# Attention plus mixture of experts on one core: the last unconditional slot computes its fourth feature block in two token parts

## The chip, the cores and the metric

The kernel runs on one core of one Trainium2 chip. The metric is the device time of one launch in microseconds (us), the median of the runs of the kernel. The engines are PE (TensorE, matmuls; PEld is its weight loading), ACT (ScalarE), DVE (VectorE), POOL (GpSimd, which here issues the indirect DMAs) and SP (which issues the plain DMAs). Each engine works through its own instructions in the order in which they were written; engines wait for each other through semaphores.

## The reference

```
scores = q @ k.T / sqrt(64) + bias(position)        # 4 batches, 8 heads, 576 tokens
x = softmax(scores) @ v  ->  (2304 tokens, 512 features)
e_idx = argmax(x @ w_gate)                          # one of 8 experts for each token
h  = relu(x[mask] @ w1[e])                          # 512 -> 1024
ye = h @ w2[e]                                      # 1024 -> 512
out[mask] = gate_w * sigmoid(x @ w_output_gate)[e] * ye
```

## The kernel before

The first 345 us or so are the attention. The rest, which the change touches, is the mixture of experts. Tokens of one expert are put into slots of CH = 288 tokens, in three groups of G = 96. SURE = 8 slots (0 to 7) are run unconditionally, by `body(s)`; further ones stand behind conditions and do not run with this input. FIRST_FEW is a small rest of 32 tokens that is computed beside slot 7.

`body(s)` has two phases. In the first, f runs over 8 blocks of 128 hidden features: 12 matmuls each (L1104), over c = 0 to 3 the pairs (w1h[c], xh), (w1h[c], xl), (w1l[c], xh). A weight is split into a rounded part and a remainder in the fp32r format: `split` lets ACT cast (L484) and then DVE subtract (L485). So the first f block reads w1h[3] in its 10th matmul and w1l[3] in its 12th. In the second phase d runs over 4 blocks of 128 output features, 24 matmuls of 288 columns each (L1125); ACT copies the block from PSUM to yt (L1131). During block d of slot s also the weight tile d of the next slot is split, and in d = 1 and 2 the next slot's tokens are transposed on PE (L513), cast on ACT (L514) and subtracted on DVE (L515).

After the four blocks the slot's answer is turned to token rows: 12 transposes (L1144) into three PSUM tiles pt, one for each group, the blocks d = 0 to 2 first, then d = 3. The tiles are copied to y by DVE, ACT, DVE (L1147) and scattered to `out` by POOL (`put`, L1069). Slot 7 writes its rows into xg[1], and its three scatters are issued at the very end of the program, groups in the order 1, 0, 2, behind the scatter of the few. PSUM tiles of the tag t (`psum_t`) rotate through three buffers; so a transpose waits until the third tile before it was read.

`slot_work` runs leftover work of the attention inside the first slots. In slot 0 this is at d = 2 and d = 3 one step each of `emit_x`: four transposes (L655) into one psum_t tile and one DVE multiplication (L664) that empties it. The third pt tile of slot 0's answer takes the buffer of the second of these.

Of the kernel before, what the change touches and what calls it, by code (L numbers as in the profile page):

```python
# [9 lines left out]
F32 = mybir.dt.float32  # L10
# [17 lines left out]
CH = 288  # L28
G = 96
# [4 lines left out]
SURE_A, SURE = 6, 8  # L34
# [98 lines left out]
def attention_moe_kernel(  # L133
# [15 lines left out]
    nc = tc.nc  # L149
    V = nc.vector  # L150
# [19 lines left out]
    def cn(name):  # L170
        o, n = _WHERE[name]
        return kept[:, o:o + n]

    ident = cn("ident")
# [8 lines left out]
    def psum_t():  # L183
        return ps_t[-1].tile([128, 512], F32, name="pt", tag="t")
# [288 lines left out]
    def load_w1(s):  # L473
        src = mw1[bass.ds(expert(s), 1)].rearrange("o (c p) f -> p (o c) f", p=128)
        for i in range(4):
            nc.sync.dma_start(out=w1r[i], in_=src[:, i, :])

    def load_w2(s):
        src = mw2[bass.ds(expert(s), 1)].rearrange("o (c p) f -> p (o c) f", p=128)
        for i in range(4):  # L480
            nc.sync.dma_start(out=w2r[i], in_=src[:, 2 * i:2 * i + 2, :])

    def split(hi, lo, src):
        nc.scalar.copy(out=hi, in_=src)  # L484
        V.tensor_tensor(out=lo, in0=src, in1=hi.bitcast(F32), op=ALU.subtract)  # L485

    def side(s):

        return s % 2 if s < SURE else 0

    def gather(s):
        part = int(s >= SURE_A)
        for j in range(1 if s == FIRST_FEW else 3):
            g = 3 * s + j
            nc.gpsimd.indirect_dma_start(
                out=xg[side(s)][j], out_offset=None, in_=x_dram[:, :] if part else x_dram[0:(B - 1) * S, :],
                in_offset=bass.IndirectOffsetOnAxis(ap=gidx[part][:, g:g + 1], axis=0),
            )

    def transpose_few():  # L500
        pt = psum_t()
        for c in range(4):
            nc.tensor.transpose(
                pt[:, c * G:c * G + G], xg[0][0][:, c * 128:c * 128 + 128], ident[0:G, 0:G]
            )
        V.tensor_copy(out=few[0], in_=pt[:, 0:4 * G].rearrange("p (c g) -> p c g", g=G)[:, :, 0:FEW])

    def transpose_x(s, c):
        xh, xl = xs[side(s)]
        xg_s = xg[side(s)]  # L510
        pt = psum_t()
        for j in range(3):
            nc.tensor.transpose(pt[:, j * G:j * G + G], xg_s[j][:, c * 128:c * 128 + 128], ident[0:G, 0:G])  # L513
        nc.scalar.copy(out=xh[:, c, :], in_=pt[:, 0:CH])  # L514
        V.tensor_tensor(out=xl[:, c, :], in0=pt[:, 0:CH], in1=xh[:, c, :].bitcast(F32), op=ALU.subtract)  # L515
        if s >= SURE:
            V.tensor_copy(out=few[0][:, c, :], in_=pt[:, 0:FEW])
# [154 lines left out]
    with ExitStack() as actx:  # L672
# [12 lines left out]
        o, n = _WHERE["psi"]  # L685
        early = hb.tile([128, 144 + 36], F32, name="early", bufs=1)
        bc, cinv = early[:, 0:144], early[:, 144:180]
        ot, n = _WHERE["tab"]
# [277 lines left out]
        for hl in range(2):  # L966
            for i, w in enumerate((wg, wog)):
                nc.sync.dma_start(
                    out=wgb[hl * 64:hl * 64 + 64, :, hl * 16 + i * 8:hl * 16 + i * 8 + 8],
                    in_=w.rearrange("(a t d) e -> t d a e", t=2, d=64)[hl],  # L970
# [24 lines left out]
        for n in range(len(pairs) + 1):  # L995
            for op in orders.get(n, ORDER).split():
                name = op.rstrip("+-")
# [54 lines left out]
    with ExitStack() as ctx:  # L1052
# [3 lines left out]
        ps2 = ctx.enter_context(tc.tile_pool(name="ps2", bufs=2, space=PSUM))  # L1056

        w2h = [wr.tile([128, 2, DM], F32R, name=f"w2h{i}") for i in range(4)]
        w2l = [wr.tile([128, 2, DM], F32R, name=f"w2l{i}") for i in range(4)]
        hh_all, hl_all = (hp.tile([128, 8, CH], F32R, name=t) for t in ("hh", "hl"))  # L1060
        hh, hl = ([t[:, i, :] for i in range(8)] for t in (hh_all, hl_all))
# [5 lines left out]
        def put(s, j, y, n=G):  # L1067
            idx = sidx[int(s >= SURE_A)][0:n, 3 * s + j:3 * s + j + 1]
            p = nc.gpsimd.indirect_dma_start(  # L1069
                out=out, out_offset=bass.IndirectOffsetOnAxis(ap=idx, axis=0),  # L1070
                in_=y[0:n], in_offset=None, bounds_check=NTOK - 1, oob_is_err=False,
            )
            for other in puts:
                tc.declare_no_dep(p.ins, other.ins, reason="no row of the answer is written twice")
            puts.append(p)
# [4 lines left out]
        def new_y(s, j):  # L1080

            if s == SURE - 1:
                return xg[1][j]
            return y2 if j == 2 else x_p.tile([128, DM], F32, name="y", tag="x")[0:G]

        def slot_work(s, at):
            for w in SLOT_WORK[s].split() if s < len(SLOT_WORK) else ():
                if w == at:
                    do_work()

        def after(s, n):

            return None if s >= SURE else s + n if s + n < SURE else FIRST_FEW if s + n == SURE else None

        def body(s):
            assert s < 5 or not (work or rows)
            xh, xl = xs[side(s)]
            for f in range(8):
                fs = slice(f * 128, f * 128 + 128)
                p1 = ps1.tile([128, 512], F32, name="p1", tag="p1")  # L1100
                n = 0
                for c in range(4):
                    for w, x in ((w1h[c], xh), (w1h[c], xl), (w1l[c], xh)):
                        nc.tensor.matmul(p1[:, 0:CH], lhsT=w[:, fs], rhs=x[:, c, :], start=n == 0, stop=n == 11)  # L1104
                        n += 1
                nc.scalar.activation(out=hh[f], in_=p1[:, 0:CH], func=ACTF.Relu)  # L1106
                V.scalar_tensor_tensor(  # L1107
                    out=hl[f], in0=p1[:, 0:CH], scalar=0.0, in1=hh[f].bitcast(F32), op0=ALU.max, op1=ALU.subtract
                )
                if f % 2 == 0:  # L1110
                    i = f // 2
                    split(w2h[i], w2l[i], w2r[i])
                slot_work(s, "f%d" % f)
            if after(s, 1):
                load_w2(after(s, 1))
            yt = yts[s % 2]
            if after(s, 1) == FIRST_FEW:
                transpose_few()
            for d in range(4):
                ds = slice(d * 128, d * 128 + 128)  # L1120
                p2 = ps2.tile([128, 512], F32, name="p2", tag="p2")
                n = 0
                for f in range(8):
                    for w, x in ((w2h, hh), (w2h, hl), (w2l, hh)):
                        nc.tensor.matmul(  # L1125
                            p2[:, 0:CH], lhsT=w[f // 2][:, f % 2, ds], rhs=x[f], start=n == 0, stop=n == 23
                        )
                        n += 1
                if after(s, 1) == s + 1:
                    split(w1h[d], w1l[d], w1r[d])  # L1130
                nc.scalar.copy(out=yt[:, d, :], in_=p2[:, 0:CH])  # L1131
                if after(s, 1) == s + 1 and d in (1, 2):
                    for c in (2 * d - 2, 2 * d - 1):
                        transpose_x(s + 1, c)
                if after(s, 1) == FIRST_FEW and d < 3:
                    (few_hidden, few_turn, few_last)[d]()
                slot_work(s, "d%d" % d)
            if after(s, 2):
                load_w1(after(s, 2))
            pts = [psum_t() for j in range(3)]  # L1140
            for d0, d1 in ((0, 3), (3, 4)):
                for j, pt in enumerate(pts):
                    for d in range(d0, d1):
                        nc.tensor.transpose(pt[0:G, d * 128:d * 128 + 128], yt[:, d, j * G:j * G + G], ident)  # L1144
            for j, pt in enumerate(pts):
                y = new_y(s, j)
                (V.tensor_copy, nc.scalar.copy, V.tensor_copy)[j](out=y, in_=pt[0:G, :])  # L1147
                if s != SURE - 1:
                    put(s, j, y)
            if after(s, 2):  # L1150
                gather(after(s, 2))

        few_h, few_ht = (yts[0].rearrange("p a b -> p (a b)")[:, 256 * i:256 * i + 256] for i in range(2))

# [43 lines left out]
        def either(s):  # L1198
            flag = ns + 1 + s
            is_small = nc.values_load(seq[int(s >= SURE_A)][0:1, flag:flag + 1], min_val=0, max_val=1)  # L1200
            with tc.If(is_small > 0) as cmp:
                small(s)
            with cmp.Else():
                body(s)

        for s in range(SURE):
            body(s)
# [44 lines left out]
```

## Time and profile before

| what | value |
|---|---|
| median of 3 runs | 593.14 us (593.07 to 593.64) |
| profiled execution, its own time | 593.73 us |
| its span in the trace | 591.9 us |
| mean granted TensorE clock (share of full speed) | 0.996 |

The span is the time between the first and the last instruction that the profiler saw; 1.8 us of the execution lie around it. Times in rows are microseconds from the start of the span.

### The profile page before, as it was taken

The page shows a single profiled execution, that of the slowest core. Times are in us where ns is not written, and L with a number is a line of the kernel's source. Part 1 is how long each engine was busy: PE and PEld are TensorE (multiplying, and loading weights), DVE is VectorE, ACT ScalarE, POOL GpSimd, SP SyncE. Part 2 cuts the span into 40 slices and gives each one's busy share as a digit, 9 for nine tenths or more (in the row PEclk, how much of TensorE's full clock was granted, in tenths as well). Part 3 has the DMA queues.
Part 4 walks back from the last instruction along what each step waited for, and adds up shares of the span by engine and source line. Part 5 has one row for each costly group of instructions (what it writes and reads, how often), then busy time and mean ns, then how long its engine had stood idle before and what let it go on. Part 6 is the DMA issues. An engine that isn't in the chain of part 4 may idle for free.

```text
span 591.9 us, 13980 instructions
## 1 busy us (share of the span) xinstructions
PE 567.2 (96%) x5294; PEld 473.7 (80%) x5294; DVE 395.7 (67%) x935; ACT 374.2 (63%) x813; POOL 106.1 (18%) x220
## 2 busy tenths in 40 slices
PE   4999899999999999999999999999999999999993
PEld 2454577777787777787787779999999999999993
DVE  5999655666866667765889846767877765565511
ACT  5998767877777777677767845444555454555411
POOL 1000111110011111011214570221222314040302
PEclk9999999999999999999999999999999999999998
DMA  6979633333224333322333765684748485766521
GB/s 136 216 205 214 164 79 71 72 72 71 49 61 114 72 72 71 112 63 48 72 102 71 264 194 172 191 263 160 232 137 245 138 246 159 208 186 211 168 69 48
DMA packets 94998, 81.41 MB, mean 138 GB/s; under 512 B 71319, under 2 KB 71575, under 8 KB 94920
## 3 DMA queue, kind: packets, MB, share of 16 engines
q1 hardware_dynamic: 88932, 66.05, 41.9%
q0 software_dynamic: 3232, 9.64, 5.2%
q10 hardware_dynamic: 2756, 4.72, 2.2%
q8 instruction: 44, 0.72, 0.5%
q14 instruction: 34, 0.28, 0.1%
HBM read 60.34 MB, written 9.50 MB: 118 GB/s over the span
## 4 chain that ended last, share of the span: by engine, by line
PE 87%; ACT 3%; DMA 3%; DVE 2%; issue 2%; SPq 1%; POOL 0%; POOLq 0%; ACTq 0%; DVEq 0%
PE p L1104 17%; PE p L1125 16%; PE pa L917 14%; PE ps L832 12%; PE pt L885 11%; PE pb L736 4%; PE pt L809 3%; PE pt L897 2%; PE pt L655 2%; DMA bias<-evh 2%; PE pt L1144 1%; PE pt L513 1%; PE pt L586 1%; ACT evh L740 1%; ACT hid L723 1%
## 5 line engine op out<-in xcount | busy, mean ns | idle before, releaser
L844 DVE CUSTOM_DVE_ANT_0 e<-ps,bias 128x576 f32<-128x576 f32 x144 | 103.9, 753 | 55.2 <-PE ps L832 51.3
L849 ACT ACTIVATE e<-e,nm 128x576 f32<-128x576 f32 x144 | 111.1, 775 | 13.6 <-DVE nm L844 13.5
L1104 PE MATMUL p<-x,w 128*128 128x288 f32 x768 | 105.8, 297 | 0.0
L1104 PEld LDWEIGHTS p<-x,w 128*128 128x128 f32 x768 | 102.8, 188 | 0.5 <-issue 0.4
L885 PE MATMUL pt<-kept,e 128*128 128x128 f32 x576 | 79.1, 278 | 0.8 <-ACT et L889 0.4
L1125 PE MATMUL p<-hh,w2h 128*128 128x288 f32 x256 | 77.3, 302 | 0.0
L889 ACT COPY et<-pt 128x512 f32<-128x512 f32 (+1 forms) x110 | 57.1, 554 | 31.8 <-PE pt L885 31.6
L1125 PE MATMUL p<-hl,w2h 128*128 128x288 f32 x256 | 75.6, 295 | 0.1
L1125 PE MATMUL p<-hh,w2l 128*128 128x288 f32 x256 | 75.3, 294 | 0.0
L917 PE MATMUL pa<-et,vt 128*64 128x256 f32 (+1 forms) x640 | 73.3, 354 | 0.2 <-DVE xt L918 0.2
L885 PEld LDWEIGHTS pt<-kept,e 128*128 128x128 f32 x576 | 63.1, 141 | 10.3 <-issue 4.4
L917 PEld LDWEIGHTS pa<-et,vt 128*64 128x64 f32 x640 | 42.9, 137 | 21.7 <-issue 7.3
L736 PE MATMUL pb<-hid,w2blk 128*32 128x288 f32 x576 | 49.5, 430 | 9.0 <-DVE hid L725 7.7
L1069 POOL DMA_INDIRECT out_dram<-y,sidx x22 | 26.3, 1198 | 173.5 <-DVE y L1147 147.2
L1106 ACT ACTIVATE hh<-p 128x288 fp32r<-128x288 f32 x64 | 26.3, 412 | 45.4 <-PE p L1104 29.5
L725 DVE TENSOR_SCALAR hid<-e,early 128x576 f32<-128x576 f32 x108 | 47.3, 514 | 4.1 <-ACT early L705 2.3
L736 PEld LDWEIGHTS pb<-hid,w2blk 128*32 128x32 f32 x576 | 22.8, 113 | 32.9 <-DVE hid L725 10.8
L485 DVE TENSOR_TENSOR w2l<-w2r,w2h 128x1024 fp32r<-128x1024 f32 x32 | 39.2, 1226 | 14.2 <-ACT w2h L484 12.7
L1125 PEld LDWEIGHTS p<-hh,w2h 128*128 128x128 f32 x256 | 48.0, 188 | 0.6 <-issue 0.6
L1125 PEld LDWEIGHTS p<-hl,w2h 128*128 128x128 f32 x256 | 48.1, 188 | 0.3 <-DVE hl L1107 0.3
L1125 PEld LDWEIGHTS p<-hh,w2l 128*128 128x128 f32 x256 | 48.2, 188 | 0.0
L832 PE MATMUL ps<-qt 64*128 64x288 f32 x256 | 46.4, 344 | 1.5 <-DVE qs L814 1.2
(222 smaller groups left out, 956.7 us busy)
## 6 DMA issues: line engine op xcount, KB each, us to landing
w1r<-in_moe_w_dram SPq DMA_DIRECT2D x36, 512.0 KB, 5.1
w2r<-in_moe_w_dram SPq DMA_DIRECT2D x36, 512.0 KB, 4.9
bias<-evh SPq DMA_DIRECT2D x16, 288.0 KB, 4.6
bias<-evl SPq DMA_DIRECT2D x16, 288.0 KB, 4.0
vt<-in_v_dram SPq DMA_DIRECT2D x16, 288.0 KB, 3.5
nat<-in_k_dram SPq DMA_DIRECT2D x32, 128.0 KB, 3.6
nat<-in_q_dram SPq DMA_DIRECT2D x32, 128.0 KB, 3.2
x_dram<-x ACTq DMA_DIRECT2D x12, 256.0 KB, 2.1
```

Source lines behind the costliest of these rows:

```text
L485: V.tensor_tensor(out=lo, in0=src, in1=hi.bitcast(F32), op=ALU.subtract)
L725: V.tensor_scalar(out=to, in0=src, scalar1=bc[:, r:r + 1], scalar2=0.0, op0=ALU.add, op1=ALU.max,)
L736: nc.tensor.matmul(pb[32 * t:32 * t + 32, c, 0:288], lhsT=w2f, rhs=hids[t][:, c * 288:c * 288 + 288], start=True, stop=True,)
L832: nc.tensor.matmul(outs[hl][:, c, 0:288], lhsT=qs[p, S + 64 + qb * 128:S + 192 + qb * 128] if qb < 4 else q4[:, t, :], rhs=keys[p, c * 288 ...
L844: V.tensor_tensor_reduce(out=e.rearrange("p (a j) -> p a j", a=2), in0=ps[:, :, 0:n], in1=bias_ap.rearrange("p (a j) -> p a j", a=2), scal ...
L849: nc.scalar.activation(out=e, in_=e, func=ACTF.Exp, scale=-1.0, bias=nm, accum_out=sum_ap)
L885: nc.tensor.transpose(pt[:, n * 256 + j * 128:n * 256 + j * 128 + 128], es[j][:, (n0 + n) * 128:(n0 + n) * 128 + 128], ident,)
L889: copy(out=et[:, n0:n0 + nn, :].rearrange("p n s -> p (n s)"), in_=pt[:, 0:nn * 256])
L917: nc.tensor.matmul(pa[p:p + 64, 0:n], lhsT=values, rhs=weights, start=i == 0, stop=i == 4)
L1069: p = nc.gpsimd.indirect_dma_start(out=out, out_offset=bass.IndirectOffsetOnAxis(ap=idx, axis=0), in_=y[0:n], in_offset=None, bounds_check ...
L1104: nc.tensor.matmul(p1[:, 0:CH], lhsT=w[:, fs], rhs=x[:, c, :], start=n == 0, stop=n == 11)
L1125: nc.tensor.matmul(p2[:, 0:CH], lhsT=w[f // 2][:, f % 2, ds], rhs=x[f], start=n == 0, stop=n == 23)
```

## The change

In slot 7 (SURE - 1) the block d = 3 is computed in two parts, first the tokens 0 to 191 (groups 0 and 1), then the tokens 192 to 287 (group 2). Between the parts the rows of groups 0 and 1 are transposed, and copied by ACT and DVE. The third group follows the second part, its copy moves from DVE to ACT. Transposing and copying are now the functions `turn` and `keep`.

A second thing changes in every slot: the copy of p2 to yt moved into the loop over the parts, which stands ahead of `split(w1h[d], ...)`; before, it stood behind it.

```
             for d in range(4):
                 ds = slice(d * 128, d * 128 + 128)
-                p2 = ps2.tile([128, 512], F32, name="p2", tag="p2")
-                n = 0
-                for f in range(8):
-                    for w, x in ((w2h, hh), (w2h, hl), (w2l, hh)):
-                        nc.tensor.matmul(
-                            p2[:, 0:CH], lhsT=w[f // 2][:, f % 2, ds], rhs=x[f], start=n == 0, stop=n == 23
-                        )
-                        n += 1
+                parts = (slice(0, 2 * G), slice(2 * G, CH)) if s == SURE - 1 and d == 3 else (slice(0, CH),)
+                for cols in parts:
+                    p2 = ps2.tile([128, 512], F32, name="p2", tag="p2")
+                    width = cols.stop - cols.start
+                    n = 0
+                    for f in range(8):
+                        for w, x in ((w2h, hh), (w2h, hl), (w2l, hh)):
+                            nc.tensor.matmul(
+                                p2[:, 0:width], lhsT=w[f // 2][:, f % 2, ds], rhs=x[f][:, cols],
+                                start=n == 0, stop=n == 23,
+                            )
+                            n += 1
+                    nc.scalar.copy(out=yt[:, d, cols], in_=p2[:, 0:width])
+                    if cols.stop == 2 * G:
+                        turn(yt, 0, 3)
+                        turn(yt, 3, 4, (0, 1))
+                        keep(s, (1, 0))
                 if after(s, 1) == s + 1:
                     split(w1h[d], w1l[d], w1r[d])
-                nc.scalar.copy(out=yt[:, d, :], in_=p2[:, 0:CH])
...
+            if s == SURE - 1:
+                turn(yt, 3, 4, (2,))
+                keep(s, (2,))
+            else:
+                turn(yt, 0, 3)
+                turn(yt, 3, 4)
+                keep(s, (0, 1, 2))
...
+        def turn(yt, d0, d1, groups=(0, 1, 2)):
+            if d0 == 0:
+                pts[:] = [psum_t() for j in range(3)]
+            for j in groups:
+                for d in range(d0, d1):
+                    nc.tensor.transpose(pts[j][0:G, d * 128:d * 128 + 128], yt[:, d, j * G:j * G + G], ident)
+
+        def keep(s, groups):
+            for j in groups:
                 y = new_y(s, j)
+                copy = V.tensor_copy if j == 0 or j == 2 and s != SURE - 1 else nc.scalar.copy
+                copy(out=y, in_=pts[j][0:G, :])
                 if s != SURE - 1:
                     put(s, j, y)
```

This is ACT's order in the second phase of slot 0, both kernels in one piece (w_0 is w1h, w1r the loaded weight, ytqt the tile yt, p the PSUM tile of a block).

```order
-L484 CAST w_0_4772<-w1r_4632 128x1024
-L1131 COPY ytqt_5119<-p_5387 128x288
-L514 CAST x<-pt 128x288 x2
-L484 CAST w_0_4772<-w1r_4633 128x1024
-L1131 COPY ytqt_5119<-p_5433 128x288
+L1133 COPY ytqt_5119<-p_5387 128x288
+L484 CAST w_0_4772<-w1r_4632 128x1024
+L514 CAST x<-pt 128x288 x2
+L1133 COPY ytqt_5119<-p_5433 128x288
+L484 CAST w_0_4772<-w1r_4633 128x1024
```

Each copy of a block moved ahead of the cast of the weight tile with the same d; the last cast now stands behind the last block's copy. The slots 1 to 6 have the same difference.

This is DVE's order at the end of slot 0 in the changed kernel (w_1 is w1l, ytqs<-pt the two steps of `emit_x`, y the rows of slot 0); apart from line numbers it is the same as before.

```order
L485 TENSOR_TENSOR w_1_4773<-w1r_4632,w_0_4772 128x1024
L515 TENSOR_TENSOR x<-pt,x 128x288 x2
L664 TENSOR_TENSOR ytqs_5120<-pt,rec 128x512
L485 TENSOR_TENSOR w_1_4773<-w1r_4633,w_0_4772 128x1024
L664 TENSOR_TENSOR ytqs_5120<-pt,rec 128x512
L1171 COPY y<-pt 96x512
L1171 COPY y_5122<-pt 96x512
L1107 SCALAR_TENSOR_TENSOR hl<-p_5514,hh 128x288
```

Nothing moved here: the subtraction that follows the last cast still stands ahead of the second L664.

This is PE's order in the changed kernel around the second part of block 3 of slot 7 (p_7878 and p_7920 are the PSUM tiles of the two parts, ytqs the tile yt).

```order
L1128 MATMUL p_7878<-hl,w2h_5112 128x192
L1128 MATMUL p_7878<-hh,w2l_5116 128x192
L1165 MATMUL pt<-kept,ytqs_5120 96x128 x11
L1128 MATMUL p_7920<-hh,w2h_5109 128x96
L1128 MATMUL p_7920<-hl,w2h_5109 128x96
...
L1128 MATMUL p_7920<-hl,w2h_5112 128x96
L1128 MATMUL p_7920<-hh,w2l_5116 128x96
L1165 MATMUL pt<-kept,ytqs_5120 96x128
```

Where 24 matmuls of 288 columns stood ahead of 12 transposes, there are 24 of 192, 11 transposes, 24 of 96 and one transpose.

## Rows read from the trace of the kernel before

**Rows 1.** Page, part 1: busy time and share of each engine.

```profile
PE 567.2 (96%) x5294; PEld 473.7 (80%) x5294; DVE 395.7 (67%) x935; ACT 374.2 (63%) x813; POOL 106.1 (18%) x220
```

**Rows 2.** Page, part 4: chain that ended last, share of the span.

```profile
PE 87%; ACT 3%; DMA 3%; DVE 2%; issue 2%; SPq 1%; POOL 0%; POOLq 0%; ACTq 0%; DVEq 0%
```

**Rows 3.** Windows: one middle slot (stretch, its length, busy time and count).

```profile
410.15:438.07 27.92, 27.92 (x218) 27.91 (x218) 20.85 (x53) 14.18 (x26) 7.21 (x6) 1.00 0.63 198
```

**Rows 4.** Timeline, end of slot 6: start, length, engine, line, operation.

```profile
538.36 0.40 ACT L1131 COPY ytqt<-p 128x288 f32<-128x288 f32 x1 [1.85 <-PE p L1125]
538.66 1.05 ACT L484 CAST w<-w1r 128x1024 fp32r<-128x1024 f32 x1
539.74 1.23 DVE L485 TENSOR_TENSOR w<-w1r,w 128x1024 fp32r<-128x1024 f32 x1 [1.97 <-ACT w L484]
...
546.14 1.07 ACT L484 CAST w<-w1r 128x1024 fp32r<-128x1024 f32 x1
...
548.99 0.40 ACT L1131 COPY ytqt<-p 128x288 f32<-128x288 f32 x1 [1.77 <-PE p L1125]
...
550.02 13.04 PE L1104 MATMUL p<-x,w 128*128 128x288 f32 x96
550.08 1.28 DVE L1147 COPY y<-pt 96x512 f32<-96x512 f32 x2 [1.61 <-PE pt L1144]
```

**Rows 5.** Timeline in slot 0: a matmul that waits for DVE.

```profile
366.10 0.45 DVE L1107 SCALAR_TENSOR_TENSOR hl<-p,hh 128x288 fp32r<-128x288 f32 x1
...
366.60 0.19 PEld L1125 LDWEIGHTS p<-hl,w2h 128*128 128x128 f32 x1 [0.32 <-DVE hl L1107]
...
366.84 0.29 PE L1125 MATMUL p<-hh,w2l 128*128 128x288 f32 x1
```

**Rows 6.** Timeline, end of slot 0 (from the answers for PE, ACT and DVE).

```profile
378.01 0.60 PE L655 MATMUL pt<-kept,xt 128*128 128x128 f32 x4
378.45 1.81 PE L1144 MATMUL pt<-kept,ytqt 128*96 128x128 f32 x12
380.01 0.77 PE L1104 MATMUL p<-x,w 128*128 128x288 f32 x4
...
378.21 0.40 ACT L1131 COPY ytqt<-p 128x288 f32<-128x288 f32 x1 [2.19 <-PE p L1125]
...
378.65 0.69 DVE L664 TENSOR_TENSOR ytqs<-pt,rec 128x512 f32<-128x512 f32 x1 [1.28 <-PE pt L655]
```

**Rows 7.** Timeline, block 3 of slot 7 and the end.

```profile
577.10 0.19 PEld L1125 LDWEIGHTS p<-hh,w2h 128*128 128x128 f32 x1 [0.20 <-issue]
...
577.21 0.19 PEld L1125 LDWEIGHTS p<-hl,w2h 128*128 128x128 f32 x1
...
577.34 0.30 PE L1125 MATMUL p<-hl,w2h 128*128 128x288 f32 x1
...
580.40 1.47 PE L1144 MATMUL pt<-kept,ytqs 128*96 128x128 f32 x12
580.60 0.40 ACT L1131 COPY ytqs<-p 128x288 f32<-128x288 f32 x1 [2.82 <-PE p L1125]
...
581.80 0.58 ACT L1147 COPY xg<-pt 96x512 f32<-96x512 f32 x1 [0.80 <-PE pt L1144]
582.66 0.92 POOL L1069 DMA_INDIRECT out_dram<-xg,sidx  x1 [3.16 <-ACT xg L1147]
...
585.11 0.92 POOL L1069 DMA_INDIRECT out_dram<-xg,sidx  x1 [0.30 <-issue]
```

**Rows 8.** Timeline: the nearest rows to matmuls and copies of few columns.

```profile
453.90 0.60 PE L413 MATMUL pt<-a,bl 128*96 128x66 bf16 x10
...
541.36 0.66 PE L513 MATMUL pt<-kept,xg 96*128 96x96 f32 x6
...
566.55 1.93 PE L1159 MATMUL p<-w1r,few 128*32 128x256 f32 x32
...
577.26 0.53 ACT L1182 COPY y<-p 32x128 f32<-32x128 f32 x2 [1.54 <-PE p L1177]
```

More of the change, by code (lines that the diff above doesn't have):

```diff
@@ L1139, in body @@
                 load_w1(after(s, 2))
[L1140 to L1145, printed above, removed]
+            if s == SURE - 1:
[5 more added lines that the diff above has]
+                keep(s, (0, 1, 2))
+            if after(s, 2):
+                gather(after(s, 2))
+        pts = []
+        def turn(yt, d0, d1, groups=(0, 1, 2)):
[6 more added lines that the diff above has]
+            for j in groups:
                 y = new_y(s, j)
-                (V.tensor_copy, nc.scalar.copy, V.tensor_copy)[j](out=y, in_=pt[0:G, :])
+                copy = V.tensor_copy if j == 0 or j == 2 and s != SURE - 1 else nc.scalar.copy
+                copy(out=y, in_=pts[j][0:G, :])
                 if s != SURE - 1:
                     put(s, j, y)
-            if after(s, 2):
-                gather(after(s, 2))
         few_h, few_ht = (yts[0].rearrange("p a b -> p (a b)")[:, 256 * i:256 * i + 256] for i in range(2))
```

## The prediction

> **What bounds the kernel now.** The page's first part shows PE busy for 96% of the span and no other engine above 67% [rows 1]; the chain that ended last runs through PE for 87% of it [rows 2]. That is an average over attention and experts, so I looked at one slot by itself: in the 27.92 us from the first matmul of slot 2 to that of slot 3 PE is busy for all 27.92, DVE for 20.85 and ACT for 14.18 [rows 3]. So in the slots PE alone sets the pace, and whatever makes PE wait is paid in full; ACT and DVE have room, but only as long as nothing that PE needs stands late in their order. At the end it is different: the last transposes are over at 581.87, and then ACT's copy, its scatter at 582.66 and two more, 1.23 us apart by (585.11 - 582.66) / 2, are all that is left [rows 7]. The part of the change that is named works there; the part that is not named works at seven slot boundaries.
>
> **Order of copy and split, slots 0 to 6.** Before, ACT cast weight tile d of the next slot while PE worked on block d: the last cast of slot 6 ran at 546.14, and w1l[3] was there by about 548.5, long before PE began the next slot at 550.02 [rows 4]. Now each cast stands behind the copy of its own block, and that copy waits for the block's last matmul. How long the pair takes after such a copy is in the rows: copy at 538.36, cast at 538.66 (0.30 later), DVE's subtraction from 539.74 to 540.97; 2.61 us from the start of the copy to the finished w1l [rows 4]. Moved to block 3 of slot 6, whose copy starts at 548.99, w1l[3] is ready at 551.60, and w1h[3] at about 550.4.
>
> Who waits? The first f block of the next slot needs w1h[3] in its 10th matmul and w1l[3] in its 12th. 96 matmuls take 13.04 us, so 0.134 each with the last one's own 0.29 taken off [rows 4, 5]. The 10th comes at 551.2: no wait. The 12th wants its weights at about 551.4: a wait. What it costs is read where a matmul waited for DVE: result at 366.55, weights at 366.60, the following matmul at 366.84, 0.29 after the result [rows 5]. So the 13th matmul starts at 551.89, where undisturbed it starts at 551.63 by the mean pace or 551.73 with the 0.24 that a first gap takes (577.10 to 577.34) [rows 7]. The loss is 0.16 to 0.26; I take 0.2. The copy and the first matmul stand 1.03 us apart at each of the boundaries 1/2 to 6/7, so it comes six times: **+1.2 us**. The bounds are 0 (DVE a little quicker than in its rows) and 0.3 each.
>
> Also behind the late subtraction in DVE's order are the two copies of y (1.28 us), then hl of the first f block. Those copies start at 551.6 and not at 550.08 [rows 4]; hl of f = 0 follows at about 553, and the fourth f block, which needs its PSUM buffer, starts at 554.8. That is covered by 1.5 us. In slots 1 to 3 leftover work of 0.8 to 1.7 us stands in between too, which leaves almost nothing in the worst of them; I cost it at 0, with 0.5 us in the range. The scatters of y and the gathers behind them on POOL, and SP's loads of w1 which overwrite what the split reads, come up to 3 us later; the data is needed a phase or more later (10 us and more).
>
> **Slot 0, the exception.** Here a step of `emit_x` stands behind the last split on DVE: four transposes at 378.01, and L664, which empties their PSUM buffer, from 378.65 to 379.34 [rows 6]. The third pt tile needs that buffer. It is already late: the 12 transposes take 1.81 us there and 1.47 in slot 7 [rows 6, 7], and PE starts the next slot 0.67 us behind the end of L664, which is the six transposes that are left (0.11 each). In the new order the subtraction of w1l[3] ends 2.61 us after the copy at 378.21, at 380.82; DVE keeps its order, so L664 (0.69, less 0.1 of overlap) ends at about 381.4 and not at 379.34. PE stands still meanwhile: **+2.1 us**. w1l[3] is there by then, so no 0.2 comes on top. As long as DVE's order stays, only a quicker cast could make it less; bounds 1.9 and 2.3.
>
> **Slot 7, block 3 in two parts.** Of the 24 matmuls of 288 columns at 0.134 there become 24 of 192 and 24 of 96. No row has fp32r matmuls so narrow, so their pace is bounded. Above: no dearer than one of 288, 0.134. Below: as the columns go; the nearest rows are six transposes of 96 columns in 0.66 us, 0.08 each after the first, and ten bf16 matmuls of 66 columns in 0.60, 0.04 each [rows 8]. What decides is whether weight loads can come closer: the second load of a block begins 0.11 after the first (577.10, 577.21), with nothing else in its way [rows 7]. So each of these matmuls, whose weights are all new, should take 0.11 or little more however narrow it is. I take 0.115 for both parts, nearest to that row.
>
> Then, from rows 7: second matmul 577.34, the 24th at 577.34 + 22 x 0.115 = 579.87, transposes from 579.99, eleven of them to 581.20; groups 0 and 1 are copied by 582.0 and scattered at 582.3 and 583.5, behind which the third scatter could go at 584.7. Second part: first at 581.20, second 0.24 later, the last at 583.97. ACT's copy 0.25 later, about 0.27 long (two of 128 columns take 0.53 [rows 8]): 584.5. Before, eleven of the twelve transposes covered this copy; now nothing does, and its single transpose takes some 0.45 with its weights: 584.94. Copy to rows 0.58, POOL 0.28 behind it: scatter at 585.80 against 585.11. **+0.7 us**: two scatters are hidden (2.45 us), but some 2.3 us of extra matmul and 1.2 us of uncovered copy and transpose take their place. With 0.11 it is +0.5, with 0.134 +1.5; by the columns (0.08 and 0.04) POOL is the limit, 584.0, -1.1. What follows the last scatter up to the end, 5.9 us, stays.
>
> **The sum.** 2.1 + 1.2 + 0.7 = +4.0 us. The profiled execution took 593.73 us, so it would take 597.7; the median of the runs is 0.59 lower, 593.14, so I forecast **597.1 us**.
>
> **Rivals.**
>
> *Narrow matmuls go by their columns.* For it: the transposes of 96 columns load 128 columns of weights each and still come 0.08 us apart [rows 8]. Against it: those are not fp32r, and the fp32r loads above are 0.11 apart. Tail -1.1, boundaries as above: +2.2, 595.3 us. The Trainium skill, "TensorE: Matmul & The Clock Gate", section "Back-to-back issue gap", also speaks for it: it gives about 81 ns for each load and matmul in a stream at 128 columns and 131 ns at 512. By an estimate between those figures (89 ns at 192, 81 at 96) the tail would be some 1.3 us less than mine, and the time 595.8. No row here has such a stream.
>
> *Narrow matmuls are dearer than wide ones*, run in two passes as plain fp32 is: the 16 matmuls that the code writes at L1159 are 32 rows [rows 8]. For it only that no fp32r row is narrower than 288 columns; 44 x 0.115 more, 602.2 us.
>
> *The new order costs nothing*, because PE meets w1l[3] just in time and L664 is somehow let through; tail +0.7: 593.8 us, no change. Against it: the order of DVE is fixed, and in slot 0 PE waits for L664 already.
>
> *The other side:* only the tail as meant, the last two matmul streams at column pace, -1.1 us, with nothing lost at the boundaries: 592.0 us. It decides only while the seven boundaries together cost less than 1.1 us; slot 0 alone has twice that.
>
> **How the numbers follow.** Forecast 0.73; column pace 0.11; two passes 0.08; no cost of the order 0.04; the other side 0.03; 0.01 for the unseen. The forecast's own spread is 596.0 to 598.6 (boundaries and pace at their bounds). The range must leave out no more than 0.2: down to the column pace, 595.0, and above the forecast's own end by what several late buffers in slots 1 to 3 would add, 599.5. Two kernels of this length can be told apart from about 0.2%, 1.2 us: faster 0.04, same 0.05, slower 0.91.
>
> **What would show it.** In the trace after: the 12 transposes at the end of slot 0 last some 3.9 us, not 1.81, with PE waiting for L664; slots 1 to 6 have one gap of 0.2 us behind the 11th matmul, with DVE's subtraction as what ended it; the subtraction of w1l[3] ends after PE began the slot. In slot 7 the narrow matmuls stand 0.11 to 0.12 apart in both parts, two scatters are issued before the second part ends, and the last about 0.7 us later against the first matmul of the block than before (8.0). The prediction is wrong if that distance shrinks by a microsecond or PE passes the end of slot 0 as before.

## The result and the profile after

| kernel | median | lowest to highest, runs |
|---|---|---|
| before | 593.21 us | 592.39 to 593.64, 6 |
| changed | 597.78 us | 595.97 to 599.86, 6 |

The ratio is 1.0073, with an interval from 1.0057 to 1.0090: the change costs 4.3 us, 3.4 to 5.3. The profiled execution of the changed kernel took 598.69 us; its span is 596.9 us against 591.9 before, +5.0, at a mean granted clock of 0.993.

Where the 5.0 us of the spans lie is found by following the same instructions through both traces. The first matmul of slot 0 starts 0.60 later (349.30 against 348.70), ahead of all that the change touches; this point moves between 347.9 and 350.8 in the profiled executions of this study and has no part in the explanation. The third f block of slot 1 (the first two are the 24 matmuls looked at below) starts 4.19 later, so the end of slot 0 cost 4.19 - 0.60 = 3.59. The first matmul of block 3 of slot 7 starts at 582.52 and not at 577.10, 5.42 later: 1.23 for the six boundaries between. From there to the end of the span it is 14.38 and not 14.80, -0.42. Spans are read to 0.1 us, so what is counted up to the end of one is good to some 0.05.

On the whole PE is as busy as before, in share [rows 1]. Page of the changed kernel, part 1:

```profile
PE 571.8 (96%) x5318; PEld 477.9 (80%) x5318; DVE 392.5 (66%) x934; ACT 374.8 (63%) x815; POOL 108.8 (18%) x220
```

**The end of slot 0** answers to [rows 6]. Timeline of the changed kernel (L1133 is the copy of a block, L1165 the transposes of the answer):

```profile
378.61 0.60 PE L655 MATMUL pt<-kept,xt 128*128 128x128 f32 x4
378.81 0.40 ACT L1133 COPY ytqt<-p 128x288 f32<-128x288 f32 x1 [2.19 <-PE p L1128]
...
379.04 0.82 PE L1165 MATMUL pt<-kept,ytqt 128*96 128x128 f32 x6
379.10 1.05 ACT L484 CAST w<-w1r 128x1024 fp32r<-128x1024 f32 x1
380.19 1.22 DVE L485 TENSOR_TENSOR w<-w1r,w 128x1024 fp32r<-128x1024 f32 x1 [1.58 <-ACT w L484]
381.33 0.68 DVE L664 TENSOR_TENSOR ytqs<-pt,rec 128x512 f32<-128x512 f32 x1
...
382.06 0.86 PE L1165 MATMUL pt<-kept,ytqt 128*96 128x128 f32 x6 [2.20 <-DVE ytqs L664]
...
382.68 4.95 PE L1104 MATMUL p<-x,w 128*128 128x288 f32 x24
```

Read it from the middle: the cast stands behind the copy now, the subtraction behind the cast, L664 behind the subtraction, and six of the twelve transposes behind L664. PE waits 2.20 for it, and slot 1 starts 33.38 after the first matmul of slot 0 and not 31.31: +2.07.

The last row holds what the prediction didn't see: the first 24 matmuls of slot 1 take 4.95. The chain that ended last has the same 24 as 4.71 us, then the next 24 and a whole first phase of slot 2:

```profile
382.92 4.71 PE p L1104 x24
388.07 3.20 PE p L1104 x24
414.33 12.98 PE p L1104 x96
```

In the kernel before the chain had for these:

```profile
380.25 3.19 PE p L1104 x24
383.88 3.20 PE p L1104 x24
...
410.15 12.78 PE p L1104 x96
```

So 1.52 us go in these 24 matmuls alone. Why is seen in the windows of the changed kernel (columns as in [rows 3]; the third number from the end is the granted clock):

```profile
381.00:382.00 1.00, 0.00 (x0) 0.00 (x0) 1.00 (x2) 0.00 (x0) 0.00 (x0) 1.00 0.07 25
382.00:383.00 1.00, 0.94 (x8) 0.94 (x9) 0.26 (x2) 0.15 (x1) 0.00 (x0) 1.00 0.48 94
383.00:384.00 1.00, 1.00 (x8) 1.00 (x7) 1.00 (x2) 0.44 (x1) 0.28 (x1) 0.75 0.89 352
384.00:385.00 1.00, 1.00 (x6) 1.00 (x5) 0.03 (x1) 0.00 (x0) 0.70 (x2) 0.50 0.20 78
385.00:386.00 1.00, 1.00 (x6) 1.00 (x6) 0.28 (x1) 0.73 (x2) 0.92 (x1) 0.50 0.65 193
386.00:387.00 1.00, 1.00 (x6) 1.00 (x6) 0.52 (x2) 0.62 (x1) 0.77 (x1) 0.54 0.54 147
387.00:388.00 1.00, 1.00 (x10) 1.00 (x10) 0.88 (x1) 0.27 (x1) 0.69 (x2) 1.00 0.50 143
```

PE stands still in 381 to 382 at full clock, works again from 382.06, and within 383 to 384 (0.75 on average) the granted clock falls to 0.50, the 1.2 GHz level, for about 3.4 us; a window counts six matmuls there instead of ten (those that reach over its edges are counted too). PE is busy through all of it, so no wait shows this loss, only the clock and the counts.

**A middle boundary** answers to [rows 4]. Timeline of the changed kernel, end of slot 6 and start of slot 7:

```profile
554.14 0.40 ACT L1133 COPY ytqt<-p 128x288 f32<-128x288 f32 x1 [1.77 <-PE p L1128]
554.43 1.05 ACT L484 CAST w<-w1r 128x1024 fp32r<-128x1024 f32 x1
555.14 1.50 PEld L1104 LDWEIGHTS p<-x,w 128*128 128x128 f32 x11
...
555.52 1.22 DVE L485 TENSOR_TENSOR w<-w1r,w 128x1024 fp32r<-128x1024 f32 x1 [1.76 <-ACT w L484]
556.66 1.28 DVE L1171 COPY y<-pt 96x512 f32<-96x512 f32 x2
556.80 1.76 PEld L1104 LDWEIGHTS p<-x,w 128*128 128x128 f32 x13 [0.15 <-DVE w L485]
```

Eleven weight loads go through, the twelfth waits for the subtraction. Over the kernel this is one line of the waits (us in total, times, longest):

```profile
PEld p L1104 <- DVE w L485: 1.0, 6, 0.2
```

**The end** answers to [rows 7]. Timeline of the changed kernel, block 3 of slot 7:

```profile
582.52 0.36 PE L1128 MATMUL p<-hh,w2h 128*128 128x192 f32 x1
...
582.72 0.28 PE L1128 MATMUL p<-hl,w2h 128*128 128x192 f32 x1
582.83 0.27 PE L1128 MATMUL p<-hh,w2l 128*128 128x192 f32 x1
...
586.53 0.28 PE L1128 MATMUL p<-hl,w2h 128*128 128x96 f32 x1
586.65 0.28 PE L1128 MATMUL p<-hh,w2l 128*128 128x96 f32 x1
...
588.76 0.92 POOL L1069 DMA_INDIRECT out_dram<-xg,sidx  x1 [0.31 <-issue]
...
589.30 0.24 ACT L1133 COPY ytqs<-p 128x96 f32<-128x96 f32 x1 [2.04 <-PE p L1128]
...
589.60 0.32 PE L1165 MATMUL pt<-kept,ytqs 128*96 128x128 f32 x1 [0.33 <-ACT ytqs L1133]
589.95 0.58 ACT L1171 COPY xg<-pt 96x512 f32<-96x512 f32 x1 [0.41 <-PE pt L1165]
590.80 0.92 POOL L1069 DMA_INDIRECT out_dram<-xg,sidx  x1 [1.12 <-ACT xg L1171]
```

Matmuls of 192 and of 96 columns stand 0.11 apart alike. Two of the three scatters go out under the second part (the second at 588.76), but the third comes 8.28 after the block's first matmul, where it was 8.01 (585.11 - 577.10), +0.27. Behind it the span lasts 6.10 us, where it was 6.79.

### The profile page after: what moved, and what is told of

It is laid out like the page before. It is cut to its first block, busy times and chain, and to the rows that moved or that the text cites. A ratio compares the mean times of both kernels' runs of the same rounds, so it can differ in the third digit from the quotient of the medians.

```text
span 596.9 us, 14028 instructions
## 1 busy us (share of the span) xinstructions
PE 571.8 (96%) x5318; PEld 477.9 (80%) x5318; DVE 392.5 (66%) x934; ACT 374.8 (63%) x815; POOL 108.8 (18%) x220
## 4 chain that ended last, share of the span: by engine, by line
PE 87%; DMA 4%; ACT 3%; issue 2%; DVE 2%; SPq 1%; POOL 1%; POOLq 0%; ACTq 0%
PE p L1104 17%; PE p L1128 16%; PE pa L917 14%; PE ps L832 12%; PE pt L885 11%; PE pb L736 5%; PE pt L809 3%; PE pt L897 2%; PE pt L655 2%; PE pt L1165 1%; PE pt L513 1%; DMA bias<-evl 1%; DMA bias<-evh 1%; PE pt L586 1%; ACT evh L740 1%
## 5 line engine op out<-in xcount | busy, mean ns | idle before, releaser
L1104 PE MATMUL p<-x,w 128*128 128x288 f32 x768 | 108.5, 300 | 0.0
L1104 PEld LDWEIGHTS p<-x,w 128*128 128x128 f32 x768 | 104.5, 191 | 1.5 <-DVE w L485 1.0
L1128 PE MATMUL p<-hh,w2h 128*128 128x288 f32 (+2 forms) x264 | 79.3, 301 | 0.0
L1128 PE MATMUL p<-hl,w2h 128*128 128x288 f32 (+2 forms) x264 | 77.6, 294 | 0.1
L1128 PE MATMUL p<-hh,w2l 128*128 128x288 f32 (+2 forms) x264 | 77.3, 293 | 0.0
L485 DVE TENSOR_TENSOR w<-w1r,w 128x1024 fp32r<-128x1024 f32 x28 | 34.3, 1225 | 51.3 <-ACT w L484 51.3
L1128 PEld LDWEIGHTS p<-hh,w2h 128*128 128x128 f32 x264 | 49.6, 188 | 0.6 <-issue 0.6
L1128 PEld LDWEIGHTS p<-hl,w2h 128*128 128x128 f32 x264 | 49.7, 188 | 0.3 <-DVE hl L1107 0.3
L1128 PEld LDWEIGHTS p<-hh,w2l 128*128 128x128 f32 x264 | 49.7, 188 | 0.0
```

The source lines that it names most:

```text
L1128: nc.tensor.matmul(p2[:, 0:width], lhsT=w[f // 2][:, f % 2, ds], rhs=x[f][:, cols], start=n == 0, stop=n == 23,)
```

## The experiments

All kernels are compared with the kernel before, run again in the same set: it took 594.38 us beside the first four kernels, 593.71 beside the next three, 593.63 and 593.81 beside the last two pairs. The theory: four things add up, namely the wait for L664 in slot 0, the slow clock behind it, six small waits, and a tail that is about even. The rivals: that the clock fell for another reason than the wait; that the narrow matmuls go by columns or are dearer, so that the tail is what moved; that the order costs nothing. The first four kernels take the change apart.

### The tail alone

Slot 7 in two parts, with copy and split in the old order in slots 0 to 6.

```
-                    nc.scalar.copy(out=yt[:, d, cols], in_=p2[:, 0:width])
+                    if s >= SURE - 1:
+                        nc.scalar.copy(out=yt[:, d, cols], in_=p2[:, 0:width])
...
                 if after(s, 1) == s + 1:
                     split(w1h[d], w1l[d], w1r[d])
+                if not (s >= SURE - 1):
+                    nc.scalar.copy(out=yt[:, d, :], in_=p2[:, 0:CH])
```

> Only the block 3 of slot 7 in two parts; copy and split of all other slots in the order of before. Theory A (read from the two traces): the whole loss lies in the new order of copy and split; the two parts bring the last scatter 0.3 us later but what follows it is 0.7 us shorter, so 0.4 us faster than before, within what can be told apart: 592.8 us. Theory B (the prediction's own term for the tail, +0.7, with the shorter end an accident of one execution): 593.9 us. If the narrow matmuls or the third copy on ACT carried the loss, it would stay near 597.8.

Measured: 593.50 us, ratio 0.9979 (0.9968 to 0.9989). All the loss is gone, so none of it is in the tail. In its profile the last scatter stands 8.28 behind the block's first matmul, as in the changed kernel, and 6.27 follow: 14.55 against 14.80, -0.25. That is less than the timing gives; the timing was repeated below.

### The order alone, in all slots, in slot 0, and in slots 1 to 6

In all three slot 7 is in one part as before. In the first the copy stands ahead of the split everywhere; in the second only in slot 0 (the condition below), in the third only in slots 1 to 6 (0 < s < SURE - 1), and behind it elsewhere.

```
-                parts = (slice(0, 2 * G), slice(2 * G, CH)) if s == SURE - 1 and d == 3 else (slice(0, CH),)
+                parts = (slice(0, CH),)
...
-                    nc.scalar.copy(out=yt[:, d, cols], in_=p2[:, 0:width])
+                    if s == 0:
+                        nc.scalar.copy(out=yt[:, d, cols], in_=p2[:, 0:width])
```

All slots: 

> Only the copy of each block ahead of the split, in all slots; slot 7 in one part as before. Theory A: 2.1 us of waiting at the end of slot 0, about 1.5 us of half clock behind it, six times 0.2 us: 4.8 us slower than before, 598.0 us, no faster than the changed kernel. Theory B: without the clock and with the tail's +0.7 gone, 3.3 us slower than before, 596.5 us.

Slot 0: 

> The copy ahead of the split in slot 0 alone. Theory A: 2.1 us of waiting and up to 1.5 us at half clock, which need not be the same in each execution: 2.1 to 3.9 us slower than before, about 596.8, with runs that lie further apart than those of before. Theory B (stall alone): 595.3 us.

Slots 1 to 6: 

> The copy ahead of the split in slots 1 to 6 alone. Both theories: six waits of 0.2 us, 1.2 us slower than before, 594.4 us, runs as close together as those of before. If the late subtraction also cost buffers in slots 1 to 3, 595 us or more.

Measured:

| order changed in | median | ratio | interval |
|---|---|---|---|
| slots 0 to 6 | 597.74 us | 1.0054 | 1.0036 to 1.0071 |
| slot 0 | 597.01 us | 1.0041 | 1.0026 to 1.0056 |
| slots 1 to 6 | 595.03 us | 1.0015 | 1.0002 to 1.0027 |

The order is the whole loss, and slot 0 more than half of it: +2.4 us (1.5 to 3.3), slots 1 to 6 +0.9 (0.1 to 1.6). The profile of slots 1 to 6 shows only the small waits, with the same line as in the changed kernel (1.0 us in six), and for L664 no more than the 0.4 us of a weight load that the kernel before has too. With the order changed in all slots, the clock fell earlier than in the changed kernel. Timeline of that kernel, end of slot 0:

```profile
377.68 0.82 PE L1161 MATMUL pt<-kept,ytqt 128*96 128x128 f32 x6
380.70 1.38 PE L1161 MATMUL pt<-kept,ytqt 128*96 128x128 f32 x6 [2.20 <-DVE ytqs L664]
```

The same wait of 2.20, but the six transposes behind it already take 1.38 and not 0.86, and the clock is 0.97 in 379 to 381 and 0.50 in 381 to 384. The 24 matmuls of the chain then take 4.24, since more of the slow stretch lies ahead of them.

### The split of slot 0's last tile behind the leftover work

The changed kernel, where in slot 0 the last split is written behind `slot_work`: L664 stands ahead of the subtraction on DVE, while the copy stays ahead of the cast.

```
-                if after(s, 1) == s + 1:
+                if after(s, 1) == s + 1 and not (s == 0 and d == 3):
                     split(w1h[d], w1l[d], w1r[d])
...
                 slot_work(s, "d%d" % d)
+                if s == 0 and d == 3:
+                    split(w1h[d], w1l[d], w1r[d])
```

> The changed kernel, but in slot 0 the split of weight tile 3 stands behind the leftover work of that block, so that the multiplication that empties the PSUM buffer is ahead of the subtraction on DVE. Theory A: no wait of 2 us at the end of slot 0, so no half clock either; what is left is six times 0.2 us (perhaps 0.2 more at the first boundary) and the tail's -0.4: 3.6 us less than the changed kernel, 594.2 us. If the wait came from the cast on ACT and not from DVE's order, nothing changes: 597.8 us.

Measured: 594.51 us, ratio 1.0007 (0.9994 to 1.0020). Timeline, from the answers for PE and DVE:

```profile
379.00 1.81 PE L1167 MATMUL pt<-kept,ytqt 128*96 128x128 f32 x12
380.56 1.71 PE L1104 MATMUL p<-x,w 128*128 128x288 f32 x11
...
379.20 0.69 DVE L664 TENSOR_TENSOR ytqs<-pt,rec 128x512 f32<-128x512 f32 x1 [0.64 <-PE pt L655]
380.27 1.23 DVE L485 TENSOR_TENSOR w<-w1r,w 128x1024 fp32r<-128x1024 f32 x1 [0.37 <-ACT w L484]
```

The twelve transposes take 1.81 again, as in [rows 6], the next 24 matmuls 3.19 at full clock. So it is the place of L664 behind the late subtraction on DVE that costs, and not the copy's place on ACT by itself; wait and slow clock go together, 4.3 - 0.4 = 3.9 us by the two timings, 3.6 by the profiles.

### Matmuls in the wait

The changed kernel, where 16 matmuls that nothing reads stand ahead of the third group's transposes in slot 0, so that PE works through the wait. They use weights that lie there, and write a free PSUM tile.

```
+                if yt is yts[0] and not filled and j == 2:
+                    filled.append(1)
+                    p2 = ps2.tile([128, 512], F32, name="p2", tag="p2")
+                    for n in range(16):
+                        nc.tensor.matmul(p2[:, 0:CH], lhsT=w2h[0][:, 0, 0:128], rhs=hh[0], start=n == 0, stop=n == 15)
```

> The changed kernel with 16 more matmuls of 288 columns (2.15 us, their result is read by nobody) between the second and the third group of transposes of slot 0, where PE waits for 2.2 us. If the half clock behind that wait comes from PE standing still (theory A), the clock stays whole, the wait itself stays paid: about 1.5 us less than the changed kernel's slower runs, 596.3 us, with runs as close together as those of before. If the clock falls for another reason, or the filler comes on top of the wait, 597.8 to 599.9 us.

Measured: 596.43 us (595.95 to 597.29), ratio 1.0046 (1.0029 to 1.0064). Timeline:

```profile
378.86 0.82 PE L1170 MATMUL pt<-kept,ytqt 128*96 128x128 f32 x6
379.43 2.35 PE L1168 MATMUL p<-hh,w2h 128*128 128x288 f32 x16
381.88 0.86 PE L1170 MATMUL pt<-kept,ytqt 128*96 128x128 f32 x6
382.50 3.43 PE L1104 MATMUL p<-x,w 128*128 128x288 f32 x24
```

Windows of this kernel, at the place where the changed kernel's clock fell:

```profile
383.00:384.00 1.00, 1.00 (x10) 1.00 (x9) 0.84 (x2) 0.25 (x1) 0.47 (x1) 1.00 0.97 397
384.00:385.00 1.00, 1.00 (x10) 1.00 (x9) 0.19 (x1) 0.64 (x2) 0.69 (x2) 1.00 0.12 45
```

Slot 1 starts 33.39 behind slot 0's first matmul, as in the changed kernel (33.38): the wait is paid in full. But the 24 matmuls take 3.43 and not 4.95, and the clock is 1.00 in every window up to 389. So the slow clock comes of PE's standing still, and not of the load of w1 or of another engine's work at that time, which stand there as in the changed kernel (the loads of w1 are issued over 4.46 us in both, from 377.30 and from 377.12).

This is one profile each; what they agree on is seen when the distance from the first matmul of slot 0 to the third f block of slot 1 is worked out from all of them:

| kernels | distance | more than before |
|---|---|---|
| before; tail alone; order in slots 1 to 6; split behind the work; the four kernels of the last two sections below | 35.18 to 35.19 us | 0 |
| matmuls in the wait | 37.25 us | 2.07 |
| changed; order in all slots; in slot 0; half the weights (below) | 38.77 to 38.82 us | 3.6 |

### Half the weights in the second part

The changed kernel, where the second part of slot 7's block 3 loads 64 columns of each weight instead of 128. It leaves out 64 features of that block for the last 96 tokens.

```
-                                p2[:, 0:width], lhsT=w[f // 2][:, f % 2, ds], rhs=x[f][:, cols],
+                                p2[0:rows_of(cols), 0:width], lhsT=w[f // 2][:, f % 2, d * 128:d * 128 + rows_of(cols)],
+                                rhs=x[f][:, cols],
...
+        def rows_of(cols):
+            return 64 if cols.start else 128
```

> The changed kernel, but the 24 matmuls of 96 columns of the second part load only 64 columns of weights, so the other 64 features of that block are left out for the last 96 tokens. Theory A (the weight load sets the pace of narrow matmuls): these 24 come 0.06 us apart instead of 0.11, the second part takes 1.2 us less, and the last scatter comes as early as POOL can issue it. Rival (a fixed cost for each matmul of this format): they stay 0.11 apart.

Measured: 596.79 us, ratio 1.0048 (1.0025 to 1.0071). Timeline of the second part:

```profile
585.39 0.22 PE L1128 MATMUL p<-hl,w2h 128*64 128x96 f32 x1
585.45 0.22 PE L1128 MATMUL p<-hh,w2l 128*64 128x96 f32 x1
585.51 0.22 PE L1128 MATMUL p<-hh,w2h 128*64 128x96 f32 x1
```

The columns that stream through are the same 96, the pace is 0.06 (0.059 over 22 of them) and not 0.111: the weight load sets it. The last scatter comes 7.47 behind the block's first matmul and is bound by POOL, its three scatters 1.23 apart; 6.05 follow it.

### What stands behind the last scatter

In the profiles the stretch from the last scatter's start to the end was 6.76 to 6.84 with the block in one part and 6.04 to 6.27 in two. The two parts also moved the last copy from DVE to ACT, so two kernels part these: the tail alone with the third copy on DVE, and the kernel before with it on ACT.

```
-                copy = V.tensor_copy if j == 0 or j == 2 and s != SURE - 1 else nc.scalar.copy
+                copy = nc.scalar.copy if j == 1 else V.tensor_copy
```

```
-                (V.tensor_copy, nc.scalar.copy, V.tensor_copy)[j](out=y, in_=pt[0:G, :])
+                (V.tensor_copy, nc.scalar.copy, nc.scalar.copy if s == SURE - 1 else V.tensor_copy)[j](out=y, in_=pt[0:G, :])
```

Third copy on DVE, two parts: 

> Slot 7's block 3 in two parts, the old order of copy and split, and the third group's rows copied by DVE instead of ACT. The question is the time from the start of the last scatter to the end of the span: 6.8 us in kernels with the block in one part, 6.0 to 6.3 in those in two parts. If the engine of the last copy decides it, it returns to about 6.8 here and the kernel loses half of what the tail alone gained (about 592.8 to 593.4). If the two parts decide it, it stays at 6.0 to 6.3 and the time is that of the tail alone (ratio about 0.998). The start of the last scatter against the first matmul of the block should stay within 0.2 of 8.28, as DVE is free there (copies of 96 x 512 take 0.64 on DVE and 0.58 on ACT).

Third copy on ACT, one part: 

> The kernel before, with one edit: the third group's rows of slot 7 are copied by ACT and not by DVE, the block stays in one part. If the engine of the last copy decides the time behind the last scatter, that falls from 6.8 to about 6.1 and the kernel is some 0.7 us faster than before (ratio about 0.999) although POOL still issues the scatters 1.23 us apart. If the two parts decide it, it stays at 6.8 and the kernel is as before (ratio 1.000).

Measured: 593.65 us, ratio 1.0000 (0.9988 to 1.0011), and 593.89 us, ratio 1.0003 (0.9990 to 1.0015). The last scatter of the first, then of the second; their spans are 591.8 and 591.6:

```profile
585.52 0.91 POOL L1069 DMA_INDIRECT out_dram<-xg,sidx  x1 [1.23 <-DVE xg L1174]
```

```profile
584.65 0.92 POOL L1069 DMA_INDIRECT out_dram<-xg,sidx  x1 [0.30 <-issue]
```

6.28 and 6.95 follow. So the copy's engine isn't it; it goes with the two parts. Nor is it that the last scatter comes alone, since with half the weights three came back to back and 6.05 followed.

The DMA packets of the traces tell where the difference lies. The last packet of the scatter ends 3.3 to 3.5 us behind the scatter's start in the five kernels with one part and 2.6 to 2.9 in the eight with two; from there to the end it is 3.4 to 3.6 in all. In the five, a 16 KB transfer of instructions (queue q8) starts 1.1 to 1.5 us behind the scatter's start and lasts 1.0 to 1.2, amid its packets; in the eight, one starts at most 0.4 behind it and the next 3.3 or more. That the transfer holds up the scatter's last packets fits all thirteen, but no run moved it, so it isn't shown.

### The tail again, and with the last copy halved

The tail alone was run a second time, beside a version in which ACT and DVE each copy half of the third group's rows.

```
+                if s == SURE - 1 and j == 2:
+                    nc.scalar.copy(out=y[:, 0:256], in_=pts[j][0:G, 0:256])
+                    V.tensor_copy(out=y[:, 256:512], in_=pts[j][0:G, 256:512])
+                else:
+                    copy(out=y, in_=pts[j][0:G, :])
```

Halved: 

> Slot 7's block 3 in two parts, old order of copy and split, and the third group's rows copied half by ACT and half by DVE (256 columns each). The chain behind the second part is copy, transpose, copy, scatter; the copy of 96 x 512 takes 0.58 on ACT, half of it some 0.3, so the last scatter should start some 8.0 after the block's first matmul and not 8.28 (tail alone) or 8.39 (third copy on DVE). By the profiles the tail is then 0.5 us shorter than before: ratio 0.999. If what the timing of the tail alone gave is real, 0.9975; if the result with DVE is, 0.9995.

Again: 

> The same kernel as the tail alone, timed a second time beside the one above. The profiles make it 0.25 us shorter behind the first matmul of block 3 than before (8.28 + 6.27 against 8.01 + 6.79), ratio 0.9996, while its first timing gave 0.9979, 0.9968 to 0.9989. If that holds, 0.998 again; if the profile's distances are all that the tail is worth, 0.9995 with an interval that takes in 1.

Measured: 593.25 us, ratio 0.9996 (0.9986 to 1.0006), and 593.48 us, ratio 0.9996 (0.9985 to 1.0007). Timeline of the halved copy:

```profile
583.79 0.37 ACT L1175 COPY xg<-pt 96x256 f32<-96x256 f32 x1 [0.41 <-PE pt L1168]
584.19 0.42 DVE L1176 COPY xg<-pt 96x256 f32<-96x256 f32 x1 [3.08 <-ACT xg L1175]
584.89 0.91 POOL L1069 DMA_INDIRECT out_dram<-xg,sidx  x1 [1.36 <-DVE xg L1176]
```

The halves didn't run side by side, DVE waited for ACT; the last scatter came 8.52 behind the block's first matmul, 0.24 later than with one copy. The second timing of the tail alone gives what its profiles say (14.55 and 14.57 against 14.80), and the first, 1.25 us, isn't repeated. Two parts without the new order are better than the changed kernel and, so far as these runs can tell, as good as the kernel before; they don't beat it for certain.

## Why the prediction was right

The forecast was 597.1 us, +4.0; measured were 597.78 us, +4.3 (3.4 to 5.3). The direction, the places and the main terms were right. One term was missed (+1.5) and one mis-sized (by 1.1 too much), with opposite signs, so that the total came out so close is in part luck.

- **Slot 0, +2.1**: +2.07, with the chain as worked out: the twelve transposes last 3.88 where 3.9 was forecast. The kernel with the split behind the leftover work shows that L664's place on DVE is the cause.
- **Six boundaries, 0.2 each, +1.2**: +1.23, at the twelfth weight load, six times. Alone +0.9 (0.1 to 1.6) was timed.
- **Late copies of y and late loads, at nothing**: right. The first phase of slot 2 has no wait but these, 12.98 against 12.78, its period is 28.12 against 27.92, and the 1.23 of all six boundaries leaves no room for more.
- **Pace of the narrow matmuls, 0.115**: 0.111 in both parts, so by the weight load. The rivals by columns and in two passes fall; half the weight columns halve the pace. The Trainium skill, "TensorE: Matmul & The Clock Gate", "LDWEIGHTS (loading the stationary operand)", has a load's time go by its weight columns, 1.2 of them in a ns. By an estimate from it that is 107 ns for 128 and 53 for 64; the rows, 111 and 59, lie 4 to 6 ns above. The 81 ns of "Back-to-back issue gap", from which the prediction made a rival, aren't seen in these fp32r streams.
- **Tail, +0.7**: mis-sized, -0.42 by the profile. Up to the last scatter it is +0.27: the pace was 0.004 lower in 44 matmuls (-0.2), and copy and transpose of the second part took 0.24 and 0.32 where 0.27 and 0.45 were put, and the eleven transposes 1.11 where 1.21 were. The summary of this term in the prediction (2.45 hidden against 2.3 and 1.2) doesn't add up to its +0.7 either; its step-by-step times do. And the sentence that what follows the last scatter stays was wrong: 6.10 and not 6.79, which lies in the scatter's own packets, for a reason that isn't shown.
- **The slow clock, not in the sum**: +1.5. The step that failed is the one that priced slot 0's wait at its own length. The matmuls behind it are slower as well, and the matmuls in the wait show that this hangs on PE's standing still.

Together: 2.07 + 1.52 + 1.23 - 0.42 = 4.4 by the profiles, against 4.3 timed. Two timings lie under their profiles, slot 0 alone with +2.4 (1.5 to 3.3) against 3.6 and all slots with +3.2 (2.1 to 4.2) against 3.6 + 1.2. Two readings of this remain, and neither is shown.

- The slow stretch may not come in every execution. The profile before has none and a mean clock of 0.996, that of the changed kernel has one and 0.993. Two of the changed kernel's six runs lie at 0.995, with spans of 594.1 and 595.0, the others at 0.988 to 0.993, with 595.5 to 598.0. But all five runs of slot 0 alone lie at 0.992 or 0.993, and a mean doesn't tell where in the kernel a stretch lay.
- The reference may have been long. The tail alone and the three orders were compared with the same runs of the kernel before, whose median was 594.38, where it was 593.21 to 593.81 otherwise. All four ratios give 0.3 to 1.6 us less than the profiles do, and the one that was timed again, the tail alone, came up by 1.0.

## What to carry to other kernels

Two lines that change places on a lightly used engine can cost more than the change that they came with: look at what stands behind the moved instruction on the next engine, here L664 behind the subtraction on DVE, and at whose buffer it empties. A wait of a busy PE is to be priced with the matmuls behind it, which may run at the lower clock; if it can't be removed, work in the wait can take that second part away, as it did here. And a block of matmuls whose weights are all new isn't shortened by cutting its columns: at 192 columns and at 96 the weight load sets the pace here, so the two parts take 0.111 for each matmul where one wide matmul takes 0.134.

## What the runs showed of the hardware

- The clock fell after PE had begun again, not in the wait: about 1.4 us after it in the changed kernel (382.06, and 0.75 on average in 383 to 384), some 0.2 us after it with the order changed in all slots (380.70, and 0.97 in 379 to 381). The wait was 2.20 in both. It stayed at the 1.2 GHz level for about 3.4 us under unbroken work, in all four profiles with this wait. The Trainium skill, "TensorE: Matmul & The Clock Gate", "HAM oscillation — how this bites in real kernels", tells of waits between groups of matmuls that leave the next group at the lower clock; here one wait did it, and the matmuls in the wait kept it off. Shorter waits do it in some executions only: in the profile of the tail alone the clock is 0.50 in 71 to 74, in the attention, behind waits of 1.16 and 0.83 us; in the kernel before, the same two waits leave it at 1.00. Six of the nine profiles without the long wait have such a stretch in the attention.
- fp32r matmuls with a new 128-column weight each come 0.111 apart at 192 and at 96 columns, 0.059 apart with 64 weight columns at 96, and 0.134 at 288 columns.
- From the start of the last scatter to the end of the span it is 6.76 to 6.95 us in five kernels that compute the last block in one part, and 6.04 to 6.31 in eight that do it in two, whichever engine made the last copy. The difference lies ahead of the end of the scatter's last packet.
